# The last stage of an attention and soft-MoE kernel: output products in plain fp32 on four row groups, combine weights turned four batches at a time, PSUM as one tile

## The chip, the cores and the metric

The kernel runs on one core of a Trainium2 chip. Its time is the device time of one execution in microseconds (us); the median of three runs of the kernel before is 619.05 us (617.65 to 619.27). The engines are PE (matrix products, with a queue PEld for the loads of the stationary operand), DVE (vector), ACT (scalar), POOL and SP (here it only issues DMAs). PE writes PSUM; ACT and DVE read it into SBUF; DMA moves SBUF to and from memory.

## The reference

Attention with a learned relative bias over 8 batches, 8 heads, 576 rows and 64 columns a head, then a soft mixture of experts with 32 slots (8 experts of 4 slots) over all 4608 tokens:

```python
attn = softmax(q @ k.T / sqrt(D) + bias) @ v        # per batch and head
x = attn.transpose(0, 2, 1, 3).reshape(4608, 512)
logits = x @ phi                                    # 4608 x 32
slot_input = softmax(logits, over tokens).T @ x     # 32 x 512
slot_out[e] = relu(slot_input[e] @ w1[e]) @ w2[e]   # per expert, 4 slots each
out = softmax(logits, over slots) @ slot_out        # 4608 x 512
```

All inputs and outputs are fp32. The last line is what the change is about: for each batch, 576 tokens by 32 combine weights times 32 by 512 slot outputs.

## The kernel before

**Main part.** 32 units (four pairs of heads, eight batches) run through scores, bias, exp, transposes and the product with v. The order of all steps of all engines is written out by hand: steady units by the offsets in `PLAIN`, the first and last ones by the list `END`; `step` and `then` give each piece of work its place, and everything runs in that order under `tc.manual_schedule()`.

**PSUM.** `ps(k)` (line 150) takes a tile of two banks, one of four pairs; the class `Banks` (line 323) takes the next free pair from the list `idle`, and `read` gives it back after as many reads as were announced. Each `Banks` so makes a new tile of the pair's place, and the framework sets the semaphores from the tiles' accesses.

**The end.** After the last unit, one core works in this order (lines 946 to 992): `turn_slots` turns the slot inputs; `first(j)` multiplies them with w1 of eight experts, in four column groups of 32 slots, and `refetch` asks for the rest of w2 in the places of used tiles; `hidden` and `turn_hidden` apply relu and turn; `second(hf, Q)` multiplies with w2, for half `hf` of the 512 output columns and half `Q` of the experts; `gather_slots(hf)` brings the 32 slots' 256 columns to all 128 partitions (four copies of the 32 rows) and leaves them in `sst`.

**The combine weights** `ck` hold, per batch, five chunks of 32 weights: four chunks of 128 tokens and one of 64. An output product is made in one pass of reduced fp32 (F32R). To keep the precision, both operands are taken apart: `split(b)` (line 861) makes on DVE a rounded copy of the weights and the residual, twice each, so that a chunk has 4 x 32 = 128 rows; `stack(b)` (line 868) turns the five chunks with five PE transposes and copies them out with ACT (`cst`, 512 columns) and DVE (`crt`, 64 columns). In `gather_slots` ACT copies the slot outputs into `sst`, rounded, and DVE (line 911) replaces the lower 64 rows by the residual. One product over 128 rows then sums the four partial products.

**The outputs.** `put(hf, b)` (line 915) makes four products, one for each chunk of 128 tokens, into the two banks of one pair; DVE copies the first bank to the output tile `ob` and ACT the second, and SP issues one DMA of 512 KB. After each second batch one more product makes the last 64 tokens of two batches, and ACT copies it to `obr`; after each fourth batch a DMA of 256 KB takes `obr` away. The homes of the `ob` tiles are places of tiles used before, 16 in all, one for each `put`. DMAs are issued by SP in program order: the weights' first, then the outputs.

Splits and stacks are placed between the puts of the first half and the two `second(1, Q)`; the puts of the second half come last, one after another.

Of the kernel before, what the change touches and what calls it, by code (L numbers as in the profile page):

```python
# [10 lines left out]
F32 = mybir.dt.float32  # L11
F32R = mybir.dt.float32r
AF = mybir.ActivationFunctionType
ALU = mybir.AluOpType
# [111 lines left out]
def body(ctx, tc, qk, v, wcol, phi, mw1, mw2, tabh, consth, out, outr):  # L126
    nc = tc.nc
    P = 128
# [4 lines left out]
    E, DM, F = mw1.shape  # L133
# [24 lines left out]
    ident = const.tile([P, P], F32, name="ident")  # L158
# [4 lines left out]
    et = xp.tile([P, 5 * P], F32, name="et", tag="et")  # L163
# [4 lines left out]
    ck = const.tile([P, B, 5, 32], F32, name="ck")  # L168
    acc = xp.tile([P, DM + P], F32, name="acc", tag="acc")
# [142 lines left out]
    def cp(eng, out, in_):  # L312
        (nc.vector.tensor_copy if eng else nc.scalar.copy)(out=out, in_=in_)  # L313
# [4 lines left out]
    for i, x in enumerate(END.split()):  # L318
        n, u = x.rstrip("+").split("/")
# [499 lines left out]
    csts, ends, hT2 = {}, {}, {}  # L819

    def refetch(*ids):
        for i in ids:
            fetch_w(homeof[i])

    def turn_slots():
        nc.vector.tensor_scalar(out=stS, in0=stS, scalar1=1e-9, scalar2=None, op0=ALU.add)
        nc.vector.reciprocal(out=stS, in_=stS)
        h = Banks()
        nc.tensor.transpose(out=h.t[:, 0, 0:P], in_=accs, identity=ident)
        sT = ends["sT"] = xp.tile([P, 4, 32], F32, name="sT", tag="ek", bufs=2)  # L830
        nc.scalar.copy(out=sT, in_=h.read()[:, 0, 0:P].rearrange("a (c s) -> a c s", c=4))
        for Q in range(2):
            nc.vector.tensor_scalar(out=sel[Q], in0=rsum, scalar1=rowm[:, Q:Q + 1], scalar2=None, op0=ALU.mult)

    def first(j):

        Q, kc = j // 4, j % 4
        if kc == 0:
            ends["h", Q] = Banks(2)
        for n in range(2):  # L840
            for g in range(4):
                nc.tensor.matmul(ends["h", Q].t[32 * g:32 * g + 32, n, :], ends["sT"][:, kc, :], wtiles[4 * j + g][n],  # L842
                                 start=kc == 0, stop=kc == 3, tile_position=(0, 32 * g))
# [14 lines left out]
        for z in range(2):  # L858
            cp(z, hT2[Q][:, 4 * z:4 * z + 4, :], h.read()[:, z].rearrange("a (x n) -> a x n", x=4))

    def split(b):

        cs = csts["s", b] = xp.tile([P, 5, 2, 2, 32], F32R, name="cs", tag=("acc", "et")[b % 2])
        ckb = ck[:, b].unsqueeze(2).to_broadcast([P, 5, 2, 32])
        nc.vector.tensor_copy(out=cs[:, :, :, 0, :], in_=ckb)
        nc.vector.tensor_tensor(out=cs[:, :, :, 1, :], in0=ckb, in1=cs[:, :, :, 0, :].bitcast(F32), op=ALU.subtract)

    def stack(b):
        if b == 0:
            csts["r"] = bsp.tile([P, 8, 64], F32R, name="crt", tag="br", bufs=1)  # L870
        if b % 2 == 0:
            csts[b] = wp.tile([P, 2, 512], F32R, name="cst", tag="w")
        cst = csts[b - b % 2][:, b % 2]
        csf = csts["s", b].bitcast(F32).rearrange("a c x y s -> a c (x y s)")
        h = Banks(2)
        pt = h.t.rearrange("a x n -> a (x n)")
        for c in range(5):
            nc.tensor.transpose(out=pt[:, c * P:(c + 1) * P], in_=csf[:, c, :], identity=ident)  # L878
        h.read()
        h.read()  # L880
        nc.scalar.copy(out=cst, in_=pt[:, 0:512])
        nc.vector.tensor_copy(out=csts["r"][:, b], in_=pt[:, 512:576])

    def second(hf, Q):

        if Q == 0:
            ends["o"] = Banks(2)
            ends["so"] = so if hf else wp.tile([P, 2, 512], F32, name="so", tag="w")
        po = ends["o"].t[:, Q, 0:256]
        for fq in range(2):  # L890
            for x in range(4):
                for g in range(4):
                    i = 32 + 16 * hf + 8 * Q + 4 * fq + g
                    nc.tensor.matmul(po[32 * g:32 * g + 32], hT2[Q][:, 4 * fq + x, 32 * g:32 * g + 32],  # L894
                                     wtiles[i][x // 2][:, 256 * (x % 2):256 * (x % 2) + 256], start=fq == 0 and x == 0,
                                     stop=fq == 1 and x == 3, tile_position=(0, 32 * g))
        ends["o"].read()
        cp(Q == 0, ends["so"][:, hf, 256 * Q:256 * Q + 256], po)
        return ends["so"]

    def gather_slots(hf):
        h = Banks()
        pf = h.t[:, 0]
        for Q in range(2):
            nc.tensor.matmul(pf[:, 0:256], sel[Q], so[:, hf, 256 * Q:256 * Q + 256], start=Q == 0, stop=Q == 1)
# [4 lines left out]
        nc.scalar.copy(out=sst, in_=pf[:, 0:256])  # L910
        nc.vector.tensor_tensor(out=sst[64:], in0=pf[64:, 0:256], in1=sst[64:].bitcast(F32), op=ALU.subtract)

    obs = {}

    def put(hf, b):

        sst = ends["sst"][:, 256 * hf:256 * hf + 256]
        pool, tag, n = homes2[8 * hf + b]
        if n == 0:
            ob = pool.tile([P, 4, 256], F32, name="ob", tag=tag)  # L920
        else:
            if n == 1:
                obs[tag] = pool.tile([P, 2, 4, 256], F32, name="ob", tag=tag)
            ob = obs[tag][:, n - 1]
        h = Banks(2)
        po = h.t.rearrange("a x (y n) -> a (x y) n", y=2)
        for c in range(4):
            nc.tensor.matmul(po[:, c, :], csts[b - b % 2][:, b % 2, c * P:(c + 1) * P], sst, start=True, stop=True)  # L928
        for z in range(2):
            h.read()  # L930
            cp(z == 0, ob[:, 2 * z:2 * z + 2, :], po[:, 2 * z:2 * z + 2, :])
        nc.sync.dma_start(out=out[b, hf], in_=ob.rearrange("p c d -> p (c d)"))
        if b % 2 == 1:
            h = Banks()
            nc.tensor.matmul(h.t[:, 0, 0:256], csts["r"][:, b - 1:b + 1].rearrange("a b n -> a (b n)"), sst, start=True,
                             stop=True)
            if b % 4 == 1:
                obs["r"] = wp.tile([P, 2, 256], F32, name="obr", tag="w")
            nc.scalar.copy(out=obs["r"][:, b // 2 % 2, :], in_=h.read()[:, 0, 0:256])
            if b % 4 == 3:  # L940
                nc.sync.dma_start(out=outr[b // 4, hf], in_=obs["r"])
# [4 lines left out]
    with tc.manual_schedule():  # L946
        for _, _, f in sorted(prog, key=lambda x: x[:2]):
            f()
        turn_slots()
        split(0)  # L950
        split(1)
# [12 lines left out]
        so = second(0, 0)  # L964
        turn_hidden(1)
        stack(0)
        second(0, 1)
        stack(1)
        split(2)
        split(3)  # L970
        gather_slots(0)
        stack(2)
        put(0, 0)
        put(0, 1)
        for b in range(2, 4):
            stack(b + 1)
            split(b + 2)
            put(0, b)
        second(1, 0)
        stack(5)  # L980
        split(6)
        put(0, 4)
        stack(6)
        split(7)
        put(0, 5)
        second(1, 1)
        stack(7)
        put(0, 6)
        gather_slots(1)
        put(0, 7)  # L990
        for b in range(8):
            put(1, b)

# [61 lines left out]
```

## Time and profile before

| what | us |
|---|---|
| median of three runs | 619.05 |
| lowest, highest | 617.65, 619.27 |
| the profiled execution | 619.4 |
| its span, first to last instruction | 617.5 |

The profile is of one execution. Its page gives each engine's busy time and share of the span, the chain of work that ended last, and the groups of instructions with count, busy time and mean. The other views used here: the busy time by stage (a row gives the stretch in us from the span's start, its length, then busy us and number of instructions for PE, PEld, DVE, ACT, POOL, then the granted PE clock, the busy share of the 16 DMA engines and GB/s); the timeline (start, length, engine, line, operation, output and inputs, form, number merged, and in brackets the idle time before and what ended it); the list of waits (who waited for whom: total us, times, longest). "128*32 128x256" means 128 rows and 32 columns of the array and a moving operand of 128 partitions by 256 elements.

### The profile page before, as it was taken

The page shows a single profiled execution, that of the slowest core. Times are in us where ns is not written, and L with a number is a line of the kernel's source. Part 1 is how long each engine was busy: PE and PEld are TensorE (multiplying, and loading weights), DVE is VectorE, ACT ScalarE, POOL GpSimd, SP SyncE. Part 2 cuts the span into 40 slices and gives each one's busy share as a digit, 9 for nine tenths or more (in the row PEclk, how much of TensorE's full clock was granted, in tenths as well). Part 3 has the DMA queues.
Part 4 walks back from the last instruction along what each step waited for, and adds up shares of the span by engine and source line. Part 5 has one row for each costly group of instructions (what it writes and reads, how often), then busy time and mean ns, then how long its engine had stood idle before and what let it go on. Part 6 is the DMA issues. An engine that isn't in the chain of part 4 may idle for free.

```text
span 617.5 us, 18782 instructions
## 1 busy us (share of the span) xinstructions
PE 586.1 (95%) x7351; PEld 379.2 (61%) x7351; DVE 423.0 (68%) x1344; ACT 473.6 (77%) x984; POOL 224.9 (36%) x336
## 2 busy tenths in 40 slices
PE   5998899999999999999999999999999999989782
PEld 3764666666666666666666666666666666544552
DVE  7997776666666766666667666686788887652442
ACT  5996888888888888888888888787886877532333
POOL 0001544545554445455544454444423344000000
PEclk9999999999999999999999999999999999999897
DMA  5778223224854454595333468323123326889738
GB/s 199 281 245 291 64 86 113 90 86 150 253 189 150 152 182 158 192 286 185 118 117 117 147 217 270 117 87 97 50 98 122 105 83 243 314 282 409 315 158 353
DMA packets 41896, 110.71 MB, mean 179 GB/s; under 512 B 7121, under 2 KB 7249, under 8 KB 41809
## 3 DMA queue, kind: packets, MB, share of 16 engines
q1 hardware_dynamic: 41808, 109.52, 52.4%
q8 instruction: 58, 0.95, 0.6%
q14 instruction: 30, 0.24, 0.1%
HBM read 82.10 MB, written 27.41 MB: 177 GB/s over the span
## 4 chain that ended last, share of the span: by engine, by line
PE 87%; ACT 4%; DVE 4%; DMA 2%; issue 1%; POOL 0%; SPq 0%; DVEq 0%; ACTq 0%; POOLq 0%
PE ps L471 25%; PE ps L368 21%; PE ps L346 16%; PE ps L258 7%; PE ps L364 6%; PE ps L894 2%; PE ps L842 2%; ACT y L388 2%; PE ps L537 1%; DMA xo<-xs 1%; PE ps L667 1%; PE ps L928 1%; PE ps L878 1%; DVE y L381 1%; DMA tabs<-in_tab_dram 1%
## 5 line engine op out<-in xcount | busy, mean ns | idle before, releaser
L310 POOL TENSOR_SCALAR y<-y,sm 128x576 f32<-128x576 f32 (+1 forms) x320 | 222.1, 707 | 303.4 <-DVE sm L397 245.1
L381 DVE CUSTOM_DVE_ANT_0 y<-ps,bm 128x576 f32<-128x576 f32 x256 | 185.3, 754 | 96.1 <-PE ps L346 59.0
L388 ACT ACTIVATE y<-y,mn 128x576 f32<-128x576 f32 x288 | 222.2, 772 | 29.5 <-DVE sm L396 18.4
L313 ACT COPY at<-ps 128x1024 f32<-128x1024 f32 (+3 forms) x211 | 153.9, 733 | 37.0 <-PE ps L346 28.0
L471 PE MATMUL ps<-at,v 128*64 128x320 f32 (+1 forms) x1280 | 175.5, 413 | 0.1
L368 PE MATMUL ps<-qk 64*128 64x288 f32 x1024 | 156.1, 421 | 0.0
L346 PEld LDWEIGHTS ps<-ident,y 64*128 64x128 f32 x2624 | 104.9, 139 | 54.6 <-POOL y L310 15.6
L346 PE MATMUL ps<-ident,y 64*128 64x64 f32 x2624 | 118.8, 227 | 4.1 <-POOL y L310 3.7
L471 PEld LDWEIGHTS ps<-at,v 128*64 128x64 f32 x1280 | 83.7, 136 | 60.2 <-issue 10.0
L368 PEld LDWEIGHTS ps<-qk 64*128 64x128 f32 x1024 | 93.2, 187 | 24.6 <-DVE sm L396 10.8
L388 ACT ACTIVATION_READ_ACCUMULATOR y<-y,mn 128x1 f32 x288 | 54.0, 188 | 0.0
L258 PE MATMUL ps<-f,wbd 128*32 128x79 f32 (+32 forms) x856 | 47.7, 348 | 3.2 <-DVE f L237 2.6
L237 DVE TENSOR_SCALAR f<-tabs,scl,nb 128x576 f32<-128x576 f32 (+17 forms) x114 | 47.9, 505 | 1.2 <-DMA tabs<-in_tab_dram 1.2
L313 DVE COPY at<-ps 128x256 f32<-128x256 f32 (+3 forms) x77 | 33.7, 441 | 18.5 <-PE ps L346 14.3
L258 PEld LDWEIGHTS ps<-f,wbd 128*32 128x32 f32 x856 | 29.6, 113 | 21.3 <-issue 10.9
L364 PE MATMUL ps<-qk 64*64 64x288 f32 x256 | 39.0, 424 | 0.0
L313 DVE COPY xts<-ps 128x256 f32<-128x256 f32 (+1 forms) x57 | 25.9, 454 | 8.5 <-PE ps L471 5.6
L262 ACT ACTIVATE e<-ps,bcon 128x591 f32<-128x591 f32 x36 | 27.0, 755 | 4.8 <-PE ps L258 3.6
L396 DVE TENSOR_SCALAR sm<-sm 128x2 f32<-128x2 f32 (+1 forms) x160 | 28.2, 176 | 3.1 <-ACT y L388 2.6
L397 DVE RECIPROCAL sm<-sm 128x2 f32<-128x2 f32 (+1 forms) x160 | 26.5, 165 | 5.5
L381 DVE CUSTOM_DVE_ANT_0 y<-ps,br 128x576 f32<-128x576 f32 x32 | 24.0, 749 | 1.5 <-PE ps L346 1.0
L381 DVE DVE_READ_ACCUMULATOR2_ANT mn<- 128x1 f32 x288 | 23.9, 83 | 0.0
(145 smaller groups left out, 361.9 us busy)
## 6 DMA issues: line engine op xcount, KB each, us to landing
wt<-in_moe_w_dram SPq DMA_DIRECT2D x63, 512.0 KB, 6.1
qk<-in_qk_dram SPq DMA_DIRECT2D x32, 608.0 KB, 3.8
v<-in_v_dram SPq DMA_DIRECT2D x32, 320.0 KB, 3.0
bias_m<-e SPq DMA_DIRECT2D x32, 295.5 KB, 4.3
out_dram<-ob SPq DMA_DIRECT2D x16, 512.0 KB, 4.0
xs<-xts SPq DMA_DIRECT2D x24, 288.0 KB, 5.5
xo<-xs SPq DMA_DIRECT2D x8, 864.0 KB, 6.4
bm<-bias_m SPq DMA_DIRECT2D x16, 288.0 KB, 3.9
```

The costliest lines, as they stand in the source:

```text
L237: nc.vector.tensor_scalar(out=f, in0=tabs[:, 0:n], scalar1=scl[:, sc:sc + 1], scalar2=nb1[:, 0:1], op0=ALU.mult, op1=ALU.max)
L258: nc.tensor.matmul(pb[32 * t:32 * t + 32, c0 // 512, c0 % 512:(c1 - 1) % 512 + 1], wbd, x, start=True, stop=True, tile_position=(0, 32 * t))
L262: nc.scalar.activation(out=e, in_=pb.rearrange("a x n -> a (x n)")[:, 0:S + 15], func=AF.Identity, bias=bc)
L310: nc.gpsimd.tensor_scalar(out=out, in0=y, scalar1=r, scalar2=1.0, op0=ALU.mult, op1=ALU.mult)
L313: (nc.vector.tensor_copy if eng else nc.scalar.copy)(out=out, in_=in_)
L346: nc.tensor.matmul(out, src[rs], ident[rs, rs], is_transpose=True, start=True, stop=True, tile_position=(64 * r, 0))
L364: nc.tensor.matmul(pss[0].t[rs, n, 0:HALF], x[rs, 1152:1216], x[rs, 64 + n * HALF:64 + (n + 1) * HALF], start=True, stop=True, tile_positi ...
L368: nc.tensor.matmul(pss[hh].t[:, n, 0:HALF], x[rs, 640 + p * P:640 + (p + 1) * P], x[rs, k0:k0 + HALF], start=True, stop=True, tile_positio ...
L381: nc.vector.tensor_tensor_reduce(out=d["y", p][:, hs].rearrange("a (x n) -> a x n", x=2), in0=t[:, :, 0:HALF], in1=biases[hp][p][:, hs].re ...
L388: nc.scalar.activation(out=y, in_=y, func=AF.Exp, bias=d["mn", p][:, hh:hh + 1], scale=-1.0, accum_out=d["sm", p][:, hh:hh + 1])
L396: nc.vector.tensor_scalar(out=r, in0=r, scalar1=1e-9, scalar2=None, op0=ALU.add)
L471: nc.tensor.matmul(po[64 * hh:64 * hh + 64], d["v"][:, v0:v0 + 64], main[:, :, 4 * hh + i, :] if i < 4 else rest, start=i == 0, stop=i == ...
```

## The change

Three things are altered.

- PSUM is one tile `psa` of eight banks, taken once; `ps(k)` is a slice of two banks of it.
- `split` is gone, and so is the residual in `gather_slots`; `sst` is plain fp32. `stack(q)` now takes four batches at a time: for each batch one transpose turns the four chunks of 32 weights at once, so that the 32 weights of chunk c stand in partitions 32c to 32c+31; four small products with the identity turn the chunks of 64 tokens. DVE copies the first bank (`cT`), ACT 64 columns of the second (`cR`).
- `put` makes its four products over 32 rows each, in the four row groups of the array, plain fp32; each goes to a bank of its own, in two pairs. Each pair is copied out by one engine, DVE or ACT. The last 64 tokens are made for four batches at once, with four products after each fourth batch.

The order at the end becomes: `stack(0)`, `second(0, 1)`, `stack(1)`, `gather_slots(0)`, eight puts, both `second(1, Q)`, `gather_slots(1)`, eight puts.

```diff
+    psa = psp.tile([P, 8, 512], F32, name="ps")
+
     def ps(k):
 
-        return psp.tile([P, 2, 512], F32, name="ps", tag=f"r{k}")
+        return psa[:, 2 * k:2 * k + 2]
...
-    def split(b):
...
+    def stack(q):
+
+        if q == 0:
+            ends["cT"] = wp.tile([P, 8, P], F32, name="cT", tag="w")
+            ends["cR"] = xp.tile([P, 2, 64], F32, name="cR", tag="acc")
         h = Banks(2)
...
+        for i in range(4):
+            nc.tensor.transpose(out=h.t[:, 0, i * P:(i + 1) * P], in_=ck[:, 4 * q + i, 0:4].rearrange("a c s -> a (c s)"),
+                                identity=ident)
+        for i in range(4):
+            nc.tensor.matmul(h.t[32 * i:32 * i + 32, 1, 0:64], ck[0:64, 4 * q + i, 4, :], ident[0:64, 0:64], start=True,
+                             stop=True, tile_position=(0, 32 * i))
+        nc.vector.tensor_copy(out=ends["cT"][:, 4 * q:4 * q + 4], in_=h.read()[:, 0].rearrange("a (b n) -> a b n", b=4))
+        nc.scalar.copy(out=ends["cR"][:, q], in_=h.read()[:, 1, 0:64])
...
-            ends["sst"] = wp.tile([P, DM], F32R, name="sst", tag="w")
-        sst = ends["sst"][:, 256 * hf:256 * hf + 256]
-        nc.scalar.copy(out=sst, in_=pf[:, 0:256])
-        nc.vector.tensor_tensor(out=sst[64:], in0=pf[64:, 0:256], in1=sst[64:].bitcast(F32), op=ALU.subtract)
+            ends["sst"] = wp.tile([P, DM], F32, name="sst", tag="w")
+        nc.scalar.copy(out=ends["sst"][:, 256 * hf:256 * hf + 256], in_=pf[:, 0:256])
...
-        h = Banks(2)
-        po = h.t.rearrange("a x (y n) -> a (x y) n", y=2)
-        for c in range(4):
-            nc.tensor.matmul(po[:, c, :], csts[b - b % 2][:, b % 2, c * P:(c + 1) * P], sst, start=True, stop=True)
         for z in range(2):
-            h.read()
-            cp(z == 0, ob[:, 2 * z:2 * z + 2, :], po[:, 2 * z:2 * z + 2, :])
+            h = Banks()
+            for y in range(2):
+                rs = slice(32 * (2 * z + y), 32 * (2 * z + y) + 32)
+                nc.tensor.matmul(h.t[:, y, 0:256], ends["cT"][rs, b, :], sst[rs], start=True, stop=True,
+                                 tile_position=(32 * (2 * z + y), 0))
+            cp(z == 0, ob[:, 2 * z:2 * z + 2, :], h.read()[:, :, 0:256])
         nc.sync.dma_start(out=out[b, hf], in_=ob.rearrange("p c d -> p (c d)"))
-        if b % 2 == 1:
+        if b % 4 == 3:
             h = Banks()
...
+            for r in range(4):
+                rs = slice(32 * r, 32 * r + 32)
+                nc.tensor.matmul(h.t[64 * (r % 2):64 * (r % 2) + 64, r // 2, 0:256], ends["cR"][rs, b // 4, :], sst[rs],
+                                 start=True, stop=True, tile_position=(32 * r, 64 * (r % 2)))
+            obr = wp.tile([P, 2, 256], F32, name="obr", tag="w")
+            nc.scalar.copy(out=obr, in_=h.read()[:, :, 0:256])
+            nc.sync.dma_start(out=outr[b // 4, hf], in_=obr)
```

More of the change, by code (lines that the diff above doesn't have):

```diff
@@ L859, in turn_hidden @@
             cp(z, hT2[Q][:, 4 * z:4 * z + 4, :], h.read()[:, z].rearrange("a (x n) -> a x n", x=4))
-    def split(b):
[L863 to L874, printed above, removed]
-        h = Banks(2)
-        pt = h.t.rearrange("a x n -> a (x n)")
-        for c in range(5):
-            nc.tensor.transpose(out=pt[:, c * P:(c + 1) * P], in_=csf[:, c, :], identity=ident)
-        h.read()
-        h.read()
-        nc.scalar.copy(out=cst, in_=pt[:, 0:512])
-        nc.vector.tensor_copy(out=csts["r"][:, b], in_=pt[:, 512:576])
+    def stack(q):
+        if q == 0:
+            ends["cT"] = wp.tile([P, 8, P], F32, name="cT", tag="w")
+            ends["cR"] = xp.tile([P, 2, 64], F32, name="cR", tag="acc")
+        h = Banks(2)
+        for i in range(4):
[6 more added lines that the diff above has]
+        nc.scalar.copy(out=ends["cR"][:, q], in_=h.read()[:, 1, 0:64])
     def second(hf, Q):
@@ L924, in put @@
             ob = obs[tag][:, n - 1]
-        h = Banks(2)
-        po = h.t.rearrange("a x (y n) -> a (x y) n", y=2)
-        for c in range(4):
-            nc.tensor.matmul(po[:, c, :], csts[b - b % 2][:, b % 2, c * P:(c + 1) * P], sst, start=True, stop=True)
         for z in range(2):
-            h.read()
-            cp(z == 0, ob[:, 2 * z:2 * z + 2, :], po[:, 2 * z:2 * z + 2, :])
+            h = Banks()
[4 more added lines that the diff above has]
+            cp(z == 0, ob[:, 2 * z:2 * z + 2, :], h.read()[:, :, 0:256])
         nc.sync.dma_start(out=out[b, hf], in_=ob.rearrange("p c d -> p (c d)"))
-        if b % 2 == 1:
+        if b % 4 == 3:
             h = Banks()
[L935 to L941, printed above, removed]
+            for r in range(4):
[5 more added lines that the diff above has]
+            nc.sync.dma_start(out=outr[b // 4, hf], in_=obr)
     homes2 = [(ldp, "qk", 0)] * 2 + [(p, t, n) for p, t in ((atp, "at0"), (atp, "at1"), (xp, "xk")) for n in (1, 2)]
@@ L949, in body @@
         turn_slots()
-        split(0)
-        split(1)
         for j in range(4):
@@ L968, in body @@
         stack(1)
-        split(2)
-        split(3)
         gather_slots(0)
[L972 to L977, printed above, removed]
-            put(0, b)
[L979 to L988, printed above, removed]
+        for b in range(8):
+            put(0, b)
+        for Q in range(2):
+            second(1, Q)
         gather_slots(1)
-        put(0, 7)
         for b in range(8):
```

## The prediction

> **What bounds the kernel now.** I read the profile's page first, then the busy time by stage, then the timeline of the last 45 us. The page:
>
> ```profile
> span 617.5 us, 18782 instructions
> PE 586.1 (95%) x7351; PEld 379.2 (61%) x7351; DVE 423.0 (68%) x1344; ACT 473.6 (77%) x984; POOL 224.9 (36%) x336
> PE 87%; ACT 4%; DVE 4%; DMA 2%; issue 1%; POOL 0%; SPq 0%; DVEq 0%; ACTq 0%; POOLq 0%
> ```
>
> The stages (us; then busy time and instructions of each engine; then granted clock, DMA share, GB/s):
>
> ```profile
> 100.00:500.00 400.00, 399.40 (x4860) 261.69 (x4858) 281.50 (x946) 339.98 (x722) 188.63 (x276) 1.00 0.46 146
> 556.00:579.00 23.00, 21.21 (x245) 11.51 (x237) 7.22 (x15) 5.42 (x10) 0.00 (x0) 1.00 1.02 407
> 577.10:584.20 7.10, 4.84 (x29) 4.21 (x30) 3.66 (x9) 3.17 (x7) 0.00 (x0) 0.85 0.72 288
> 584.20:588.50 4.30, 4.30 (x66) 2.16 (x66) 1.36 (x3) 0.86 (x2) 0.00 (x0) 0.85 0.55 225
> 588.50:592.50 4.00, 2.53 (x19) 2.15 (x19) 2.13 (x5) 1.49 (x3) 0.00 (x0) 1.00 0.14 54
> 592.50:596.20 3.70, 3.70 (x66) 2.04 (x66) 1.71 (x4) 1.03 (x3) 0.00 (x0) 1.00 0.45 176
> 596.20:599.80 3.60, 2.64 (x21) 2.33 (x19) 1.28 (x4) 1.82 (x4) 0.00 (x0) 1.00 0.28 115
> 602.00:615.70 13.70, 4.13 (x25) 3.23 (x23) 3.96 (x6) 5.11 (x11) 0.00 (x0) 0.77 1.01 399
> ```
>
> In the long middle PE is busy for 399.4 of 400 us: nothing of the change is there except the way PSUM is allocated. The change's work lies after 568 us, and there three things bound in turn: PE, with DMA full beside it (407 GB/s until 579 us, all of it weights, since the first output is issued at 579.20, below); from 577 to 600 us nothing fully (PE works 4.84+4.30+2.53+3.70+2.64 = 18.0 of 22.7 us, DMA falls to 54 GB/s); from 602 to 615.7 us the output DMA at 399 GB/s, with PE nearly done. What I read from this: the end is set by when the second half's outputs begin to flow, plus their bytes.
>
> **The path through that hole.** The timeline:
>
> ```profile
> 569.50 3.18 PEld L894 LDWEIGHTS ps<-wt,hT 128*32 128x32 f32 x64 [0.37 <-ACT hT L313]
> 573.09 0.76 PE L878 MATMUL ps<-ident,cs 128*128 128x128 f32 x5
> 573.69 1.03 PE L905 MATMUL ps<-so,sel 128*128 128x256 f32 x4
> 574.76 0.37 ACT L910 CAST sst<-ps 128x256 fp32r<-128x256 f32 x1 [0.28 <-PE ps L905]
> 576.61 0.43 DVE L911 TENSOR_TENSOR sst<-ps,sst 64x256 fp32r<-64x256 f32 x1
> 577.09 1.22 PE L928 MATMUL ps<-sst,cst 128*128 128x256 f32 x8 [0.55 <-DVE sst L911]
> 579.20 7.37 SPq L932 DMA_DIRECT2D out_dram<-ob  x4
> 584.19 4.27 PE L894 MATMUL ps<-wt,hT 128*32 128x256 f32 x64
> 592.55 3.66 PE L894 MATMUL ps<-wt,hT 128*32 128x256 f32 x64
> 602.00 3.93 SPq L932 DMA_DIRECT2D out_dram<-ob  x4
> 611.87 1.13 SPq L941 DMA_DIRECT2D out_dram<-obr  x1
> ```
>
> `gather_slots(0)` has its ACT copy at 575.13, but the residual on DVE (L911) comes at 576.61, because `split(2)` and `split(3)` stand before it in DVE's order. `put(0, 0)` starts at 577.09. The first output of the second half, `put(1, 0)`, is issued at 602.00.
>
> **Removed, added, moved.** The groups of the stretch from 573 us on (count | busy us, mean ns):
>
> ```profile
> L928 PE MATMUL ps<-sst,cst 128*128 128x256 f32 x64 | 11.4, 312 | 1.8 <-DVE sst L911 1.5 <-ACT ob L313 0.3
> L313 DVE COPY ob<-ps 128x512 f32<-128x512 f32 x16 | 10.6, 686 | 1.3 <-DMA wt<-in_moe_w_dram 0.5 <-PE ps L928 0.4 <-issue 0.3
> L313 ACT COPY ob<-ps 128x512 f32<-128x512 f32 x16 | 9.4, 587 | 11.2 <-DVE ob L313 9.6 <-DMA wt<-in_moe_w_dram 1.4
> L878 PE MATMUL ps<-ident,cs 128*128 128x128 f32 x35 | 5.7, 299 | 4.6 <-DVE cs L866 4.6
> L881 ACT CAST cst<-ps 128x512 fp32r<-128x512 f32 x7 | 4.1, 590 | 4.9 <-PE ps L878 4.9
> L866 DVE TENSOR_TENSOR cs<-ck,cs 128x320 fp32r<-128x320 f32 x6 | 2.9, 491 | 0.2
> L865 DVE CAST cs<-ck 128x320 fp32r<-128x320 f32 x6 | 2.9, 477 | 0.0
> L911 DVE TENSOR_TENSOR sst<-ps,sst 64x256 fp32r<-64x256 f32 x2 | 0.9, 428 | 1.0 <-ACT sst L910 0.9
> ```
>
> Gone: all splits (12 here, 5.8 us of DVE), L911, the 40 stack transposes with their waits on DVE (4.6 us), and six of the seven late stack copies on ACT and on DVE. Added: per `stack(q)` four transposes and four small products. Five transposes took 0.76 us, so four take about 0.6; the small products I price at 0.3 by the nearest row, the 32-column products of L679 below (40 in 1.43 us, 0.036 each, two instructions a product); from 0 to 0.9 us if they don't overlap. So a stack is 0.9 us instead of 0.76. The first has a cover, the 0.37 us for which PE waits at 569.5 for ACT's `hT` copy (without it, +0.15); the second stands on the path: +0.15.
>
> What a new `put` costs PE is not in the trace. Nearest rows:
>
> ```profile
> 549.25 10.51 PE L842 MATMUL ps<-wt,sT 128*32 128x512 f32 x96 [0.92 <-ACT sT L831]
> 257.86 1.24 PE L368 MATMUL ps<-qk 64*128 64x288 f32 x8
> 546.10 1.43 PE L679 MATMUL ps<-xk,ek 128*32 128x128 f32 x40
> 600.64 1.29 DVE L313 COPY ob<-ps 128x512 f32<-128x512 f32 x2 [0.18 <-PE ps L928]
> 601.36 1.19 ACT L313 COPY ob<-ps 128x512 f32<-128x512 f32 x2
> DMA to landing us min/median/max: 2.6/4.0/5.0
> ```
>
> A plain fp32 product is two instructions; on the full array one of 256 columns takes (1.03-0.38)/3 = 0.217 us from start to start (L905). A put is four products, eight instructions: 1.74 us one after another, 0.87 two side by side, 0.43 four side by side. L842 has 512 columns, 0.43 us alone by the same rate, and 96 in 10.51 us are 0.11 each: four column groups run side by side. L368 has two row groups of 64: eight of 288 columns would take about 2.1 us in turn and take 1.24, so row groups run side by side too. I take 0.43 and keep 0.87 and 1.74.
>
> The Trainium skill speaks against 0.43: "TensorE: Matmul & The Clock Gate", section "LDWEIGHTS (loading the stationary operand)", prices a load by its columns alone, whatever the rows; eight loads of 128 columns would by its formula be an estimated 0.85 us a put if they ran in turn. The L368 row goes against running in turn, since its loads of 128 columns fit inside 1.24 us with two row groups; by the page's price the result is that of the 0.87 case below.
>
> At 0.43 PE is not the limit of a put; the copies are: DVE 1.29/2 = 0.65 us and ACT 0.60 us, now from two PSUM pairs, so ACT need not wait for DVE (9.6 us of such waits now). ACT also has two `obr` copies of the same shape each half. First half: 10 x 0.60 = 6.0 us.
>
> The sum on the trace's own axis:
> - `stack(1)` and gather: 573.09 + 0.9 + 1.03 = 575.0; ACT copy and hand-over 0.45: `put(0, 0)` at 575.5 instead of 577.09.
> - eight puts, 6.0: 581.5. The weights that `second(1, .)` needs are in by 579.
> - `second(1, 0)`, `second(1, 1)`: 2 x 3.66, and 0.5 because the second now follows the first directly and, if the two halves of a pair stay ordered, waits for DVE's copy: 589.3.
> - `so` copy, gather's second half, `sst` copy: 0.45 + 0.6 + 0.45: 590.8.
> - `put(1, 0)`: 0.6 for its products, 0.7 for copies, 0.2 for the issue: output issued at 592.3 instead of 602.00.
> - DMA: a half is 8 x 512 KB + 2 x 256 KB = 4.72 MB, 11.8 us at 399 GB/s. The first half's begin behind the weights at about 579 and end at 590.8, so the queue is free at 592.3. An output lands 2.6 us after issue at the least (the row of landings), of which 1.3 are its bytes: 592.3 + 1.3 + 11.8 = 605.4. Now the last issue, 611.87, plus the median 4.0 gives 615.9, 1.6 before the end: 607.0.
>
> So span 617.5 becomes 607.0, a gain of 10.5. The profiled execution took 619.4 us, 1.9 around its span and 0.35 above the median of 619.05; on the median the forecast is **608.6 us**. What is late next is the output DMA: with no hole in it from 579 on, the end could not be before 579 + 23.6 + 1.9 = 604.5 span, 606.1 on the median, where that is the forecast's floor.
>
> **PSUM as one tile.** The trace shows how instructions of different engines on one PSUM tile are ordered:
>
> ```profile
> DVE crt L882 <- ACT cst L881: 12.3, 7, 4.2
> ACT ob L313 <- DVE ob L313: 9.6, 7, 1.9
> ```
>
> `cst` and `crt` are read from different banks of one pair and written to different tiles, and still DVE waits for ACT. The program, not the data, orders them. If that is because a tile handed back as a whole needs its last reader to know of the other readers, a tile that is never handed back loses the wait. If the unit of ordering is the tile, one tile of eight banks orders every PSUM access of PE, ACT and DVE in the whole kernel. The Trainium skill, "PSUM — Partial Sum Buffer", section on bank collisions, asks for order only within a bank and quadrant; so the chip would not need the wider one.
>
> **Rivals.**
> *Slower: the tile is the unit of ordering.* Then PE stands still during each read of PSUM. The reads are
>
> ```profile
> L381 DVE CUSTOM_DVE_ANT_0 y<-ps,bm 128x576 f32<-128x576 f32 x256 | 185.3, 754 | 96.1 <-PE ps L346 59.0
> L313 ACT COPY at<-ps 128x1024 f32<-128x1024 f32 (+3 forms) x211 | 153.9, 733 | 37.0 <-PE ps L346 28.0
> ```
>
> and with PE's 586.1 these two alone make 925 us. It decides as soon as the order reaches across pairs. For it: the two wait rows. Against: they are all inside pairs that are taken and given back. Chance 0.13.
> *Slower: the row groups run in turn.* 1.74 us a put, over the DMA's 1.3: the first half is 10 groups, 17.4 us, to 592.9; seconds and gather to 602.2; 17.4 more to 619.6; copy 0.7, landing 2.6, end 1.6: 624.5 span, 626 on the median. Decides from 1.3 us a put. Against: L368. Chance 0.04.
> *Faster by less.* Two groups side by side or loads in turn, 0.87: first half 8.7 instead of 6.0, second half still DMA's, 611.3. Or the granted clock drops as now (0.85 from 577 to 588; 4.27 us instead of 3.66 for one `second`): +0.6 to +2. Or order within pairs delays more copies. 610.5 to 616; chance 0.11.
> *No change:* the outputs flow no earlier, for example since they wait for buffers or DMA lanes; I see no such wait in the rows. Chance 0.03.
>
> **How the numbers follow.** Forecast 606 to 610.5: 0.69. The range leaves out the two slower rivals and no change, 0.2: 605.5 to 616. Faster 0.80; within 0.3%, about what a measurement of this kernel can tell from no change, 0.03; slower 0.17.
>
> **What would show it.** PE between 100 and 500 us still 399 us busy: the PSUM step right; if DVE and ACT show waits on one another there, wrong. `put(0, 0)` at about 575.5, `put(1, 0)` issued near 592.3, eight products of a put within 0.6 us, ACT's output copies free of DVE, DMA near 400 GB/s from 579 with a gap of at most 2 us. Weights landing after 581, or puts spaced by more than 0.9 us, would prove the sum wrong.

## The result and the profile after

The kernel after takes 607.94 us (median of four runs, 607.13 to 608.45), the kernel before, run beside it, 619.16 us (617.65 to 619.8): a ratio of 0.9821, 95% interval 0.98 to 0.9842, or 11.1 us. The profiled execution took 607.81 us, its span is 605.4 us. The forecast was 608.6. Of the executions reported below, one (old order, 618.12 us) showed a lower mean clock, 0.977 against 0.989 to 0.995 in the five others of its kernel, and is left out of its time.

From the page of the kernel after (span; busy time of each engine; shares of the chain that ended last):

```profile
span 605.4 us, 18911 instructions
PE 582.2 (96%) x7423; PEld 370.5 (61%) x7423; DVE 414.9 (69%) x1320; ACT 469.8 (78%) x974; POOL 224.6 (37%) x336
PE 83%; DMA 6%; DVE 4%; ACT 3%; issue 1%; POOL 0%; SPq 0%; DVEq 0%; ACTq 0%; POOLq 0%
```

Busy time by stage of the kernel after (columns as before the prediction: stretch, length, busy us and instructions of PE, PEld, DVE, ACT, POOL, granted clock, DMA share, GB/s):

```profile
100.00:500.00 400.00, 399.29 (x4880) 258.03 (x4878) 282.63 (x948) 341.57 (x724) 190.13 (x279) 1.00 0.46 147
573.30:580.50 7.20, 6.35 (x80) 3.35 (x80) 5.15 (x8) 5.18 (x9) 0.00 (x0) 1.00 1.03 410
580.50:587.60 7.10, 7.10 (x133) 4.08 (x129) 0.42 (x1) 0.59 (x1) 0.00 (x0) 1.00 1.02 412
587.60:589.30 1.70, 1.24 (x8) 0.57 (x4) 0.00 (x0) 0.74 (x2) 0.00 (x0) 1.00 0.80 319
589.30:590.90 1.60, 1.15 (x17) 0.73 (x17) 0.75 (x2) 0.79 (x2) 0.00 (x0) 1.00 0.25 100
590.90:603.70 12.80, 5.35 (x64) 2.65 (x64) 4.41 (x7) 4.94 (x9) 0.00 (x0) 0.88 0.93 370
```

In the middle PE looks as before, 399.3 of 400 us busy, but it starts 4880 instructions there instead of 4860: more work in the same time. That is the first thing that the forecast had not. In the end the DMA runs at 410 GB/s through puts and seconds and then has one hole: it is below 300 GB/s from 588.5 to about 592 us, 3.5 us where the forecast allowed 2. Before, its mean was below 300 GB/s in each stage from 577 to 600.

The timeline of the end (start, length, engine, line, operation, form, number, idle time before and what ended it):

```profile
570.84 0.66 PE L870 MATMUL ps<-ident,ck 128*128 128x128 f32 x4
573.27 1.15 PE L921 MATMUL ps<-sst,cT 32*128 32x256 f32 x16 [0.46 <-ACT sst L903]
574.07 1.29 DVE L315 COPY ob<-ps 128x512 f32<-128x512 f32 x2 [1.40 <-PE ps L921]
574.82 1.31 PE L921 MATMUL ps<-sst,cT 32*128 32x256 f32 x16 [0.41 <-DVE ob L315]
575.57 1.29 DVE L315 COPY ob<-ps 128x512 f32<-128x512 f32 x2 [0.21 <-PE ps L921]
577.71 1.29 DVE L315 COPY ob<-ps 128x512 f32<-128x512 f32 x2 [0.85 <-DMA wt<-in_moe_w_dram]
579.20 1.29 DVE L315 COPY ob<-ps 128x512 f32<-128x512 f32 x2 [0.21 <-PE ps L921]
580.54 7.11 PE L888 MATMUL ps<-wt,hT 128*32 128x256 f32 x128
584.34 0.42 DVE L315 COPY so<-ps 128x256 f32<-128x256 f32 x1 [3.85 <-PE ps L888]
589.30 1.15 PE L921 MATMUL ps<-sst,cT 32*128 32x256 f32 x16 [0.46 <-ACT sst L903]
590.91 2.99 SPq L924 DMA_DIRECT2D out_dram<-ob  x4
593.86 1.29 DVE L315 COPY ob<-ps 128x512 f32<-128x512 f32 x2 [0.87 <-PE ps L921]
599.72 1.12 SPq L933 DMA_DIRECT2D out_dram<-obr  x1
```

The path reads as forecast: `stack(1)`, gather, eight puts, two seconds in a row, gather, `put(1, 0)`, bytes. Two puts, 8 products or 16 instructions, take 1.15 us to the end of the last: the row groups work side by side. DVE's copy of `so` (584.34) no longer stops PE. But PE waits for a pair (0.41 at 574.82) and DVE for data (0.21, 0.85): the puts are slower than forecast. The 0.85 is put down to a DMA of weights; the same wait in the second half (593.86, 0.87) ends with PE's products, so it is read as a wait for PE here too.

To compare kernels stage by stage I use five marks that all of them have, counted in the trace. *Way*: from the start of PE's 1500th matrix instruction to that of its 6500th, from about 115 to 525 us, the same instructions everywhere. *First*: the first product with w1. Then `put(0, 0)`, the issue of the first output of the second half, and the end of the span.

| kernel | way | first at | first to put(0,0) | to issue | to end | first to end |
|---|---|---|---|---|---|---|
| before | 410.37 | 549.25 | 27.84 | 24.92 | 15.48 | 68.24 |
| after | 409.07 | 547.06 | 26.21 | 17.64 | 14.53 | 58.38 |
| after, pairs taken anew | 410.35 | 548.47 | 26.27 | 18.25 | 16.17 | 60.68 |
| after, four lasting pairs | 409.05 | 546.27 | 26.27 | 18.46 | 15.90 | 60.64 |
| before, one tile | 409.05 | 549.68 | 27.03 | 19.71 | 15.47 | 62.21 |
| before, splits early | 410.33 | 548.48 | 26.40 | 23.49 | 15.48 | 65.37 |
| before, one tile, splits early | 409.31 | 547.79 | 26.20 | 19.23 | 15.46 | 60.89 |
| after, old order | 409.31 | 547.89 | 26.21 | 17.50 | 15.14 | 58.84 |
| after, interleaved | 409.05 | 547.01 | 26.21 | 17.99 | 14.40 | 58.59 |
| after, double puts | 409.05 | 548.21 | 26.21 | 16.89 | 14.71 | 57.81 |

The start of *first* scatters by more than the way explains (546.3 to 549.7 among kernels with one tile): the first 115 us differ from one execution to the next. So a whole time tells apart about 1 us, the stages in most cases less. They are not free of it: in the run below that leaves out half of the second half's DMAs, whose code is the same up to there, *first* to `put(0, 0)` took 27.90 us instead of 26.21, since PE worked on *first* at a granted clock of 0.67 (547 to 550 us) and 0.76 (550 to 553) instead of 1.00.

### The profile page after: what moved, and what is told of

Read it like the earlier page. It is cut to its first block, busy times and chain, and to the rows that moved or that the text cites. A ratio compares the mean times of both kernels' runs of the same rounds, so it can differ in the third digit from the quotient of the medians.

```text
span 605.4 us, 18911 instructions
## 1 busy us (share of the span) xinstructions
PE 582.2 (96%) x7423; PEld 370.5 (61%) x7423; DVE 414.9 (69%) x1320; ACT 469.8 (78%) x974; POOL 224.6 (37%) x336
## 4 chain that ended last, share of the span: by engine, by line
PE 83%; DMA 6%; DVE 4%; ACT 3%; issue 1%; POOL 0%; SPq 0%; DVEq 0%; ACTq 0%; POOLq 0%
PE ps L473 25%; PE ps L370 21%; PE ps L348 17%; PE ps L260 7%; PE ps L366 6%; DMA wt<-in_moe_w_dram 5%; ACT y L390 2%; PE ps L539 1%; DMA xo<-xs 1%; PE ps L669 1%; PE ps L888 1%; DVE ob L315 1%; PE ps L921 1%; DVE y L383 0%; POOL y L312 0%
## 5 line engine op out<-in xcount | busy, mean ns | idle before, releaser
L348 PEld LDWEIGHTS ps<-ident,y 64*128 64x128 f32 x2624 | 103.1, 139 | 56.5 <-POOL y L312 16.0
L370 PEld LDWEIGHTS ps<-qk 64*128 64x128 f32 x1024 | 90.8, 188 | 26.7 <-DVE sm L398 9.8
L260 PEld LDWEIGHTS ps<-f,wbd 128*32 128x32 f32 x856 | 33.2, 112 | 16.9 <-issue 8.1
```

The source lines that it names most:

```text
L260: nc.tensor.matmul(pb[32 * t:32 * t + 32, c0 // 512, c0 % 512:(c1 - 1) % 512 + 1], wbd, x, start=True, stop=True, tile_position=(0, 32 * t))
L348: nc.tensor.matmul(out, src[rs], ident[rs, rs], is_transpose=True, start=True, stop=True, tile_position=(64 * r, 0))
L370: nc.tensor.matmul(pss[hh].t[:, n, 0:HALF], x[rs, 640 + p * P:640 + (p + 1) * P], x[rs, k0:k0 + HALF], start=True, stop=True, tile_positio ...
```

## The experiments

### Which part of the change is worth what

Both parts alone. The kernel after with pairs taken anew:

```diff
-    psa = psp.tile([P, 8, 512], F32, name="ps")
-
     def ps(k):
 
-        return psa[:, 2 * k:2 * k + 2]
+        return psp.tile([P, 2, 512], F32, name="ps", tag=f"r{k}")
```

> The kernel after, with the PSUM pairs taken as new tiles again; all else as after. Theory (one tile is worth something everywhere, since a pair taken as a new tile makes PE wait for its own earlier work and the two engines that read one pair are put in order): the first products of the end start 2.2 us later again (549.2 instead of 547.1), 0.3 to 1 us more are lost at the end, 610.3 to 611.3 us. Rival (the 2.2 us come from something else, the end alone changed): 607.6 to 608.3.

Measured: 610.99 us (609.97 to 611.66), ratio to the kernel before 0.9865 (0.9841 to 0.9889). The theory holds for the size, less well for the parts: *first* starts 1.4 us later, not 2.2, of which 1.3 are the way; the end is 2.30 us longer, but 1.64 of these come after the issue, with a DMA engine that is late (last section), and only 0.66 before it.

The kernel before with the same lines the other way round, one tile and nothing else:

> The kernel before, with PSUM as one tile and nothing else. Theory (order by banks instead of by pairs): 2.2 us gained before the end begins, and 0.5 to 1.5 us in the end, where ACT's copy of the weights' four chunks and DVE's of the fifth chunk, and the two halves of an output, no longer wait for each other: 615.3 to 616.5 us. Rival (no effect without the other parts): 618.5 to 619.5. The recorded rival (one tile orders all of PSUM): 925 or more.

Measured: 611.59 us (611.11 to 613.69), ratio 0.9886 (0.986 to 0.9911). This is 4 us better than the theory, and nothing of the recorded rival is there. One tile alone gives 7.1 us (0.0114 of 618.9), the rest of the change alone 8.4 (with the 1.64 us of the late DMA engine against it, if the profiled execution stands for all), both together 11.1: they remove partly the same waits. The list of waits of the kernel before from 573 to 603 us (who waited for whom: us, times, longest):

```profile
DVE crt L882 <- ACT cst L881: 12.3, 7, 4.2
ACT ob L313 <- DVE ob L313: 9.5, 6, 1.9
PE ps L878 <- DVE cs L866: 4.6, 3, 2.0
PE ps L928 <- DVE sst L911: 1.5, 2, 1.0
```

and of the kernel before with one tile:

```profile
DVE crt L884 <- PE ps L880: 8.0, 5, 4.0
PE ps L880 <- DVE cs L868: 2.1, 3, 0.9
ACT ob L315 <- PE ps L930: 1.2, 2, 0.9
PE ps L930 <- DVE sst L913: 0.9, 2, 0.6
```

DVE no longer waits for ACT's copy of `cst`, it waits for the data itself; so its splits come earlier (the fifth, counted from *first*, at 29.7 instead of 32.1 us) and PE's wait for them falls from 4.6 to 2.1 us. The order of ACT behind DVE in the outputs is gone. One tile shortens the old end by 6.03 us (62.21 against 68.24), of the 9.86 us that lie between before and after. That the program's order inside a pair is what it removes there is argued from these two lists: the kernel before with four lasting pairs was not run.

### What is it in the one tile?

PSUM as four tiles of two banks, taken once and kept, in the kernel after:

```diff
-    psa = psp.tile([P, 8, 512], F32, name="ps")
+    psk = [psp.tile([P, 2, 512], F32, name="ps", tag=f"r{k}") for k in range(4)]
 
     def ps(k):
 
-        return psa[:, 2 * k:2 * k + 2]
+        return psk[k]
```

> The kernel after, with PSUM as four tiles of two banks, each taken once and kept, instead of one tile of eight banks. Theory (what costs is that a tile is taken and given back, not how many banks it has): PE's way from its 1500th to its 6500th product takes 409.05 us as in the kernels with one tile (410.35 in those that take pairs anew), and the whole 607.5 to 608.6 us. Rival (the eight banks in one tile matter): 410.35 on that way and 610.3 to 611.7 us.

Measured: 609.99 us (608.68 to 611.07), ratio 0.9871 (0.9853 to 0.989); the way 409.05. The theory is right on the way and wrong on the time, which lies between the two ranges. The way depends on whether a tile is taken anew: with lasting tiles it is 1.0 to 1.3 us shorter, whatever their size. What differs there shows in the groups of the scores' line, for the kernel before and for this one (instructions of PE's load queue that only wait: number, duration in ns, first and last start):

```profile
L368 PEldq EVENT_SEMAPHORE  x80: 51/51/51, 53.2 to 504.3; - x80
```

```profile
L370 PEldq EVENT_SEMAPHORE  x32: 51/51/51, 53.6 to 502.3; - x32
```

With pairs taken anew 48 loads at this line wait for the semaphore that PE's own products raise, with lasting tiles none; DVE's semaphore, for which they have to wait too, is then waited for by 48 instructions of their own, so that 80 do nothing but wait instead of 32. That these waits are the 1.3 us is argued, not shown. The end, however, is that of the pairs, 60.64 us: 0.88 us more than after up to the issue and 1.37 behind it (last section). The list of waits of this kernel from 546 to 607 us, and its timeline:

```profile
DVE hS L851 <- ACT hS L850: 11.0, 2, 7.9
DVE hT L315 <- ACT hT L315: 3.1, 2, 1.9
ACT cR L876 <- DVE cT L875: 2.5, 2, 1.4
```

```profile
579.81 3.66 PE L888 MATMUL ps<-wt,hT 128*32 128x256 f32 x64
583.61 0.42 DVE L315 COPY so<-ps 128x256 f32<-128x256 f32 x1 [3.84 <-PE ps L888]
584.09 3.66 PE L888 MATMUL ps<-wt,hT 128*32 128x256 f32 x64 [0.61 <-DVE so L315]
```

The two engines that read different banks of a pair are in order again, and `second(1, 1)` waits 0.61 us for DVE's copy out of the other bank. So in a lasting tile of two banks readers of different banks are ordered, and in the tile of eight banks, in slices, they are not; the prediction's guess that a tile that is never handed back loses the wait does not hold for two banks. Why the framework orders the wider tile more finely, and whether by banks or by slices, stays open.

### Are late splits what the old end lost?

The kernel before, with places for four split weights instead of two and each split two stacks ahead:

```diff
-        cs = csts["s", b] = xp.tile([P, 5, 2, 2, 32], F32R, name="cs", tag=("acc", "et")[b % 2])
+        cs = csts["s", b] = xp.tile([P, 5, 2, 2, 32], F32R, name="cs", tag=("acc", "et", "lp", "c3")[b % 4])
...
-        split(0)
-        split(1)
+        for b in range(4):
+            split(b)
...
-        split(2)
-        split(3)
         gather_slots(0)
+        split(4)
+        split(5)
...
-            split(b + 2)
+            split(b + 4)
```

(`split(6)` and `split(7)` between the later puts go too.)

> The kernel before, pairs as tiles, reduced fp32, with the splits moved two stacks ahead (four places for split weights instead of two), so that no stack and no residual waits for DVE's splits. Theory (late splits are most of what the old end loses): put(0, 0) 1 us earlier, 4.6 us of PE's waits gone, 613 to 615.5 us. Rival (the loss is PE's own work of the old form, 40 transposes and products of 0.31 us, and the order inside pairs): 617 to 619.

Measured: 616.66 us (615.24 to 620.05), ratio 0.9971 (0.9949 to 0.9992): 1.8 us, between the two. The list of waits from 573 to 603 us says why:

```profile
DVE crt L882 <- ACT cst L881: 12.8, 6, 4.2
ACT ob L313 <- DVE ob L313: 10.1, 7, 2.6
PE ps L894 <- ACT ob L313: 1.5, 1, 1.5
PE ps L928 <- DVE sst L911: 1.3, 2, 1.0
PE ps L878 <- DVE crt L882: 0.9, 1, 0.9
```

PE waits no more for `cs`, but now for ACT's output copies and DVE's `crt` copies, which stand behind each other as before: other waits take up part of the gain.

The same with one tile:

> The kernel before with both: PSUM as one tile and the splits two stacks ahead; the arithmetic in reduced fp32 stays. Theory (with one tile the only waits left in the old end are the 2.1 us of PE for late splits and 1 us of the residual; the rest is PE's own work): put(1, 0) 1.5 to 2.5 us earlier than with one tile alone, 609.0 to 610.3 us, so that the new arithmetic itself is worth 1 to 2.5 us. Rival (early splits are worth as little as in the kernel before or nothing, other waits take their place): 611 to 612.

Measured: 610.26 us (609.1 to 611.41), ratio 0.987 (0.985 to 0.989), the theory's upper edge; `put(1, 0)` comes 1.31 us earlier after *first*, a little less than the theory's 1.5 to 2.5, and first to end falls from 62.21 to 60.89 us. What is then left for the new arithmetic and its order is 60.89 - 58.38 = 2.5 us in the stages, and 0.987 - 0.9821 or 3 us in the times. Of the 2.5 us 0.93 lie behind the issue; there the old order alone costs the kernel after 0.61 (15.14 against 14.53, below).

### Do the row groups make the put cheap?

All four products of a put in the first row group:

```diff
-                rs = slice(32 * (2 * z + y), 32 * (2 * z + y) + 32)
+                rs = slice(0, 32)
...
-                                 tile_position=(32 * (2 * z + y), 0))
+                                 tile_position=(0, 0))
```

> The kernel after, but all four products of a put stand in the first row group of the array (32 rows, always chunk 0 of the weights, so the outputs of the other chunks are not computed). Theory (the four row groups work side by side, and that is what makes a put cheap on PE): the eight instructions of a put run in turn, 0.217 us each, 1.74 us a put; the first eight puts take 15 us instead of 7.3, put(1, 0) is issued near 600, and the second half is paced by PE: 617.5 to 621 us. Rival (copies pace the puts anyway, the row groups are worth nothing): 607.5 to 609.

Measured: 646.23 us (644.44 to 647.74), ratio 1.0447 (1.0412 to 1.0482). The rival falls. The theory's direction holds, its size does not. Busy time by stage of this kernel, the first puts and then the rest of them:

```profile
575.40:577.90 2.50, 2.48 (x11) 2.14 (x12) 0.69 (x1) 0.45 (x1) 0.00 (x0) 0.99 1.04 411
577.90:587.00 9.10, 9.10 (x22) 6.66 (x20) 2.08 (x3) 1.31 (x3) 0.00 (x0) 0.50 0.66 263
588.10:602.00 13.90, 13.90 (x36) 10.44 (x32) 2.77 (x4) 2.35 (x4) 0.00 (x0) 0.50 0.42 170
```

At full clock an instruction starts 0.216 us after the one before, as worked out. After 2.5 us the granted clock falls to 0.50 and the next starts after 0.43 us, so eight puts take 27.7 us (575.42 to 603.09) instead of 15. In the kernel after, the clock stays at 1.00 over the same puts.

### What sets the end?

Two runs leave out output DMAs of the kernel after: first every second one of 512 KB in the second half (the 256 KB ones stay), then all of the first half.

> The kernel after, leaving out the output DMAs of every second batch in the second half (2.1 of its 4.72 MB). Theory (the end is put(1, 0) plus the bytes): 5.2 us of bytes go, but the last 256 KB are only issued near 598, 602.5 to 603.5 us. Rival (the copies and issues of the last puts set the end): 606.5 to 608.

Measured: 603.55 us (601.68 to 605.94), ratio 0.9748 (0.971 to 0.9787), just over the theory's upper edge. From the issue to the end it takes 9.51 us instead of 14.53, 5.0 of the 5.2 us of bytes: the bytes are the tail.

> The kernel after, leaving out all output DMAs of the first half (4.72 MB). Theory (these bytes are through before put(1, 0) is issued, the end is that issue plus the second half's bytes): no change, 607.3 to 608.5 us. Rival (the second half's bytes queue behind the first's): 602 to 606.

Measured: 607.68 us (606.56 to 608.16), ratio 0.9822: the first half's 4.72 MB cost nothing.

### Can put(1, 0) come earlier?

Three versions. The order of before (`second(1, 0)` after the fourth put, `second(1, 1)` after the sixth):

> The kernel after with the order of before: second(1, 0) after the fourth put, second(1, 1) after the sixth, gather before the last put of the first half. Theory (puts are paced by the copies, PE has 3 us to spare among the eight puts, and a second between them uses it): put(1, 0) is issued 1.5 to 2.5 us earlier than 590.9, 605.6 to 606.6 us. Rival (the new order itself brought the gain, the puts of the first half first and both seconds behind them): 609 or more. Third (the copies wait behind second's products as they did before): 607.5 to 608.5.

Measured: 608.62 us (five executions, 606.13 to 609.52), ratio 0.9824 (0.9792 to 0.9857). Neither the theory nor the rival holds, and the third range is missed by 0.1 us: the old order gains 0.14 us up to the issue (17.50 against 17.64) and loses 0.61 behind it, so the new order by itself is worth nothing that the times can tell.

The seconds in pieces between the puts:

```diff
-        for b in range(8):
+        parts = iter(range(16))
+        for b, n in enumerate((1, 2, 2, 2, 2, 2, 2, 3)):
             put(0, b)
-        for Q in range(2):
-            second(1, Q)
+            for _ in range(n):
+                second_part(next(parts))
         gather_slots(1)
```

(`second_part(i)` is four products of the loop in `second`, with the copy after the 8th and the 16th.)

> The kernel after with the 16 pieces of both second(1, .) placed between the eight puts of the first half, 1, 2, 2, 2, 2, 2, 2, 3. Theory (from 573 us on the time is set by PE's puts and seconds in a row, then by the output bytes; the hole in the DMA at 588 to 591 us is worth 2 to 2.5 us): put(1, 0) issued near 587.2, no hole, end set by DMA alone: 605.3 to 606.2 us. Rival (the hole is not what the end waits for): 607.5 to 608.3. Other rival (weights of second land too late for the pieces and stop the puts): 608 to 610.

Measured: 608.32 us (607.18 to 610.18), ratio 0.9828 (0.9802 to 0.9854). A miss: the output is issued 17.99 us after `put(0, 0)`, not 14. The timeline of PE's loads shows what took the place of the copies:

```profile
576.39 0.31 PEld L936 LDWEIGHTS ps<-sst,cT 32*128 32x128 f32 x8 [0.41 <-ACT ob L315]
577.04 0.59 PEld L903 LDWEIGHTS ps<-wt,hT 128*32 128x32 f32 x16 [0.33 <-issue]
578.04 0.31 PEld L936 LDWEIGHTS ps<-sst,cT 32*128 32x128 f32 x8 [0.41 <-ACT ob L315]
```

At every change between products of 32 rows and of 128 rows the next load starts 0.33 to 0.41 us late, 15 times from 573 to 588 us; with it a put and two pieces take 1.65 us (576.39 to 578.04), where 0.43 for the put and 0.89 for the pieces (2 x 7.11/16) make 1.3. The Trainium skill says so in "TensorEngine Tiling (Array Packing)", section "Key Properties": changing the tiling mode drains the array. The trace agrees. The 0.41 is put down to ACT's copy in these lines, but it is the same in two others (574.42 and 580.27) where no engine's copy ended it.

Puts 2 to 7 of the first half two at a time, two batches in the two halves of the same banks, with one copy of 1024 columns by each engine:

```diff
...
+        for z in range(2):
+            h = Banks()
+            for n in range(2):
+                for y in range(2):
+                    rs = slice(32 * (2 * z + y), 32 * (2 * z + y) + 32)
+                    nc.tensor.matmul(h.t[:, y, 256 * n:256 * n + 256], ends["cT"][rs, b + n, :], sst[rs], start=True,
+                                     stop=True, tile_position=(32 * (2 * z + y), 0))
+            cp(z == 0, ob[:, :, 2 * z:2 * z + 2, :].rearrange("p n y d -> p y n d"),
+               h.read().rearrange("p y (n d) -> p y n d", n=2))
...
```

> The kernel after, with the puts 2 to 7 of the first half made two at a time: two batches share the banks (columns 0 to 255 and 256 to 511), one copy of 1024 columns by each engine for two batches, so that four puts are in flight instead of two. Theory (the eight puts take 7.3 us instead of the forecast's 6.0 since a pair is refilled too late for the copying engine): they take 5.6 to 6.2 us, put(1, 0) is issued 1 to 1.5 us earlier than 590.9, 606.3 to 607.0 us. Rival (the copies' own time paces them, or the end does not wait for put(1, 0)): 607.6 to 608.3.

Measured: 608.4 us (606.88 to 610.95), ratio 0.9838 (0.9809 to 0.9868). The timeline from the first put to the seconds:

```profile
574.42 1.15 PE L921 MATMUL ps<-sst,cT 32*128 32x256 f32 x16 [0.46 <-ACT sst L903]
575.97 1.16 PE L945 MATMUL ps<-sst,cT 32*128 32x256 f32 x16 [0.40 <-DVE ob L315]
577.65 2.77 PE L945 MATMUL ps<-sst,cT 32*128 32x256 f32 x32
580.94 0.42 PE L888 MATMUL ps<-wt,hT 128*32 128x256 f32 x4
```

The eight puts take 6.52 us instead of 7.27, not the theory's 5.6 to 6.2; the issue comes 0.75 us earlier, first to end is 0.57 us shorter. How much of the 0.75 is the late refill of a pair stays open: one copy of 1024 columns is also cheaper than two of 512 (DVE 1.22 against 2 x 0.69 us, ACT 1.02 against 2 x 0.59), which is worth 0.45 to 0.5 us over the three double puts. That is below what the times resolve. No version beats the kernel after by a difference that can be measured.

## Why the prediction was right, point by point

**The time is right, its owners are partly wrong.** The forecast gave all 10.5 us to the end without splits and stacks, and counted the PSUM step at nothing but a risk. Measured, that step alone gives 7.1 us, the rest alone 8.4. The step that failed is the reading of the middle, "PE is busy for 399.4 of 400 us: nothing of the change is there except the way PSUM is allocated": a full row does not say that the work in it can't be done in less time. It was worth 1.30 us on the way, and the sign named for it (PE still 399 us busy) came true, 399.29, and told nothing. In the end the forecast saw the right rows (`crt` behind `cst`, `ob` behind `ob`) and asked whether one tile loses such waits or makes them worse, but gave only the second a price. It took the end without them for granted, since the products go to two pairs; with pairs as tiles the waits stay in `hidden`, `turn_hidden`, `stack` and `second`, where they cost 0.88 us up to the issue (0.06 and 0.82 between the rows of after and of four lasting pairs).

**Which put comes when.** `put(0, 0)`, forecast 575.5, came at 573.27: 1.30 us of the 2.2 are the way, the rest is *first* starting earlier, within the scatter of executions. From *first* on the forecast is (575.5 - 549.25) = 26.25 us, measured 26.21. `stack(1)`, gather and `sst`: forecast 2.38, measured 2.43 (570.84 to 573.27).

**A put on PE.** 0.43 us was taken, and two puts have their 16 loads in 0.74 us:

```profile
573.27 0.74 PEld L921 LDWEIGHTS ps<-sst,cT 32*128 32x128 f32 x16 [0.86 <-ACT sst L903]
```

or 0.37 a put, though one load takes 0.18. From 573.59 us on, groups of four products start 0.216 us apart, 0.43 a put, the four within 0.02 us. The Trainium skill says that a load's price goes by its columns, not its rows ("TensorE: Matmul & The Clock Gate", "LDWEIGHTS (loading the stationary operand)"); the trace agrees for one load, 0.18 us with 32 rows and 0.19 with 128 (L935 of the kernel before). Over four row groups the loads do not add up, so the 0.85 that stood against the forecast does not come about here. In turn a put would have been 8 x 0.216 = 1.73, shown by the run in one row group at full clock.

**The eight puts: mis-sized.** 10 x 0.60 = 6.0 were forecast, 7.27 measured (573.27 to 580.54). The sum took ACT with ten copies, busy throughout. The timeline adds up by DVE: 0.80 us until its first copy begins (573.27 to 574.07), which the sum had not, eight copies of 0.645 or 5.16, and gaps of 0.21, 0.85 and 0.20 between them. With four puts in flight and larger copies it is 6.52. A put takes 0.91 us in the mean (7.27/8, the products of the last tokens included), just over the 0.9 that the prediction named as a sign of a wrong sum: here the sum was wrong, by 1.27 us.

**The seconds: mis-sized the other way.** 7.82 forecast, 7.11 measured. The 0.5 kept for order within a pair was not due with one tile; with four lasting pairs it is 0.61.

**From there to the end: right.** From the seconds' end to the issue 3.0 forecast, 3.26 measured (587.65 to 590.91); from the issue to the end 14.7 forecast, 14.53 measured. Summed up, the issue came at 590.91 instead of 592.3: 2.2 us earlier by `put(0, 0)`, 1.3 later by the puts, 0.7 earlier by the seconds, 0.3 later by the tail. That the last three nearly cancel, and that 0.9 of the 2.2 us is scatter, is luck; the time as a whole is nearer to the forecast (0.7 us) than its terms are.

**The rivals.** "The tile is the unit of ordering" fell with both kernels that have one tile: spans of 605.4 and 611.9 us, where the reads of PSUM in a row with PE would take 925. "Row groups in turn" fell. Of "faster by less", neither two groups at a time (a put takes 0.43 us) nor a lower clock (1.00 from 573.3 to 590.9 us) came. "The outputs flow no earlier" fell: they are issued at 590.91 instead of 602.00.

## What to carry to other kernels

In this kernel PSUM tiles taken anew for each use cost time that no busy row shows; look for instructions that only wait, and for engines that wait for each other although they read different banks, and try lasting tiles before any arithmetic is changed. When two parts of a change remove the same waits, each alone shows most of the gain (7.1 and 8.4 of 11.1 us): only a table with both, either and none says what each is worth. Work that is put into an engine's gaps pays for each change of the array's mode, so fine interleaving can give back all that it gains, as here (17.99 against 17.64 us to the issue).

## What the runs showed of the hardware that was not expected

**The clock.** In one row group PE was busy 9.10 of 9.10 us and its granted clock still fell from 0.99 to 0.50. The Trainium skill ("TensorE: Matmul & The Clock Gate", "What's actually happening") makes the rate follow from how busy the array has been recently, full when busy; here a quarter of its rows, busy all the time, was not enough. Which measure of activity decides was not tried.

**One late DMA engine.** The two kernels with pairs and the new end need 16.17 and 15.90 us from the issue to the end in their profiled executions, the kernel after 14.53. The DMA view from 591 us on, for four lasting pairs (40 slices of 0.4 us; then the queue of instruction loads: packets, MB, share) and for the kernel after (slices of 0.375 us):

```profile
GB/s 0 0 399 399 420 400 399 399 389 430 399 399 410 399 379 343 466 369 384 389 420 394 399 400 420 399 400 430 399 364 389 169 20 26 26 10 0 0 0 20
q8 instruction: 1, 0.02, 0.3%
```

```profile
GB/s 16 44 393 404 437 372 404 393 404 415 393 426 382 415 415 333 415 399 437 415 371 437 382 415 426 360 437 393 404 426 415 339 404 98 0 0 0 22 0 0
```

With the four pairs 20 to 26 GB/s are left for the last 1.4 us, a sixteenth of 400: one of the 16 engines is late. There a load of 16 KB of instructions falls among the outputs, while in the kernel after that load ends before `put(1, 0)` and only 8 KB fall there. In all ten other kernels whose outputs run at full rate, the kernel after among them, no load of 16 KB begins between that issue and the last bytes, and the last one or two engines are alone for at most 0.25 us. That the load makes the engine late is argued from this coincidence, not shown: the trace does not name the late engine, the load takes 0.88 us and the engine is about 1.5 us late, and no run moved the load.
